# Row maxima and row sums of an attention from PSUM, in turned 32x32 blocks, in place of extra matmuls

## The chip, the cores and the metric

The kernel runs on one core of a Trainium2 chip. The metric is the device time of one execution in microseconds (us), the median of several runs; less is better. The profile comes from one execution on the chip.

## The reference, cut to what matters

A retention layer (a decaying linear attention, `_attn_ref`) gives `x` of shape (4, 768, 512). On it stands a mixture of four attention experts. Each expert is a causal softmax attention with head size 64, and the two experts with the largest gate are mixed.

```python
for e in range(E):                       # E = 4, S = 768, Hd = 64
    q = x @ wq[e]; k = x @ wk[e]; v = x @ wv[e]
    scores = scale * (q @ k.transpose(0, 2, 1))
    causal = np.triu(np.ones((S, S), dtype=bool), 1)
    scores = np.where(causal, -1000000000.0, scores)
    scores = scores - scores.max(-1, keepdims=True)
    a = np.exp(scores)
    a /= a.sum(-1, keepdims=True) + 1e-09
    ye = a @ v @ wo[e]
    for kk in range(K):                  # K = 2, topk from x @ w_gate
        mask = topk[:, :, kk] == e
        out += mask[..., None] * w[:, :, kk:kk + 1] * ye
```

## The kernel before, in words

**Tiling.** Each of the 4 sequences is cut into two halves of 384 rows; the 8 halves are numbered j = 0 to 7 (`NJ`). A half has 3 chunks of 128 rows (`CH`, `C`). The experts come in two pairs p, with e = 0 or 1 inside a pair. An odd half attends to 6 blocks of 128 keys (its own 3 and the 3 of the half before it), an even half to 3.

**Three streams.** `stream_r` runs the retention, chunk after chunk (`h1`, `h2`: L336, L340, L395, L401, with VectorE work on L350, L366 and L409). `stream_p` projects half j to queries and keys (`proj`, 12 matmuls of 384 columns each on L567, split by ScalarE and VectorE into a high part k1 and a low part q2/k2, L572 and L575, and moved between partitions by DMAs issued by SP on L584), makes values and gate logits (`vgate`, L609), the row maxima (`mpass`, `mrow`) and the gate (`gate`, `gate2`). `stream_a` does the attention of half j: `score`, `av` (L862), `norm_a` or `norm_last`, `wout` (L975). While stream r is at half s, stream p is at s-1 and stream a at s-2; the last two attentions follow at the end.

**Row maxima before.** `mpass(j, p, e, i)` multiplies the 128 queries of chunk i with the keys, so that the queries lie on the partitions: L690 (384 keys of the half before, odd halves, i > 0), L703 (the same for i = 0), L704 (the own (i + 1) * 128 keys). VectorE takes the maximum along the free dimension, on L693 with a plain reduction and on L712 with a reduction that also adds the causal mask `cmask`. `mrow` turns the six columns of maxima by a matmul with the identity (L740), ScalarE takes them negated to SBUF (L742), and two DMAs of SP bring them to row 64 of q2 (L744, L746). For j = 7 `mrow` does it by matmuls instead (L733, L736).

**Scores before.** `score(j, p, kb)` multiplies with the keys on the partitions and the queries along the free dimension. Each bank gets two matmuls per expert: L816 (k1 with q1, 128 rows) and L817 (k2 with q2, 65 rows: the low parts, and a row of ones in k2 against the negated maxima in q2). ScalarE takes the exponential into `pt` (L823). GpSimd zeroes the upper triangle of diagonal blocks (L829) and adds the key blocks up into `ac` (L838, L845; VectorE for j = 7). `norm_f` sums `ac` over the partitions by 24 matmuls of 128 columns with a selector `sel` (L886); VectorE adds 1e-9, takes the reciprocal and multiplies with the gate weights (L892, L896, L897). DMAs spread the result (L908, L912).

**What sets the order.** All work is recorded as operations with an engine and dependencies. A tuple `ORDER` written into the file says in which order they are issued (each engine executes its own in that order), and `SLOTS` which buffer of each ring an operation uses. Six PSUM banks form the ring `ps`, which projections, values, retention, maxima, scores and outputs share; one more bank is `ps_o` (output of `av`), one `ps_st` (retention state).

## Time and profile before

| what | us |
|---|---|
| median of 3 runs | 322.73 (322.45 to 324.85) |
| profiled execution: span from first to last instruction | 321.6 |
| profiled execution: its own time | not listed apart; the runs' median is 1.1 above the span |
| TensorE matmuls busy (PE) | 314.9 |
| VectorE busy (DVE) | 175.6 |
| GpSimd busy (POOL) | 167.9 |
| ScalarE busy (ACT) | 128.7 |

In the rows below PE is TensorE's matmuls, PEld its weight loads, DVE VectorE, ACT ScalarE, POOL GpSimd, SP the engine that issues the DMAs. A row of a group gives line, engine, operation, output<-input, shapes, count, then busy time in us, mean ns of one, and the idle time of the engine before them with what ended it. Matmuls overlap in their pipeline, so the mean of one is longer than the distance from one to the next; the chain of waits gives that distance.

### The profile page before, as it was taken

How to read it: one execution, taken by the hardware profiler on the slowest of the kernel's cores; microseconds unless marked ns; L12 is line 12 of the kernel's file. 1: busy time of each engine (PE TensorE's matmuls, PEld its weight loads, DVE VectorE, ACT ScalarE, POOL GpSimd, SP SyncE). 2: the span in 40 equal slices, each digit the busy share in tenths (PEclk: the TensorE clock that was granted, in tenths of full speed). 3: DMA queues.
4: the chain of work that ended last, by engine and by line, in shares of the span. 5: the costliest groups of instructions: out<-in, count | busy, mean ns of one | idle time of the engine just before them, and what ended most of it. 6: DMA issues, size and time to landing. Idle time of an engine off the chain costs nothing.

```text
span 321.6 us, 10842 instructions
## 1 busy us (share of the span) xinstructions
PE 314.9 (98%) x4552; PEld 272.5 (85%) x4552; DVE 175.6 (55%) x465; ACT 128.7 (40%) x322; POOL 167.9 (52%) x205
## 2 busy tenths in 40 slices
PE   8899999999999999999999999999999999999995
PEld 3699998889978799979978789987979798987764
DVE  1672675868344166765323453865525325886842
ACT  1242323343534334342535233334344433547643
POOL 1647232665893904581479923393198454562500
PEclk9999999999999999999999999999999999999999
DMA  7996677844846518440767624843622413435022
GB/s 272 312 395 192 190 225 201 240 119 154 229 128 218 212 45 244 98 129 2 215 173 234 245 96 93 231 139 100 240 73 61 108 28 104 132 106 169 0 99 101
DMA packets 22501, 51.07 MB, mean 159 GB/s; under 512 B 3794, under 2 KB 8742, under 8 KB 22452
## 3 DMA queue, kind: packets, MB, share of 16 engines
q1 hardware_dynamic: 22452, 50.38, 51.2%
q8 instruction: 36, 0.59, 0.8%
q14 instruction: 13, 0.11, 0.1%
HBM read 30.99 MB, written 6.79 MB: 117 GB/s over the span
## 4 chain that ended last, share of the span: by engine, by line
PE 95%; DMA 2%; SPq 1%; DVE 0%; issue 0%; ACT 0%; ACTq 0%
PE ps L567 21%; PE ps L609 11%; PE ps_o L862 11%; PE ps L975 11%; PE ps L816 7%; PE ps L817 7%; PE ps_st L336 5%; PE ps L401 5%; PE ps L704 4%; DMA qkT_t<-in_qkT_dram 2%; PE ps L886 2%; PE ps L690 2%; PE ps L395 2%; PE ps L340 2%; PE ps_st L862 1%; PE ps L703 1%
## 5 line engine op out<-in xcount | busy, mean ns | idle before, releaser
L823 ACT ACTIVATE pt<-ps 128x384 f32<-128x384 f32 (+2 forms) x112 | 50.2, 490 | 29.4 <-PE ps L817 26.4
L829 POOL TENSOR_SCALAR_AFFINE_SELECT pt<-pt 128x256 f32<-128x256 f32 x48 | 19.7, 419 | 67.9 <-ACT pt L823 67.5
L712 DVE CUSTOM_DVE_ANT_0 scr<-ps,cmask_t 128x128 bf16<-128x128 f32 (+3 forms) x64 | 30.2, 486 | 26.6 <-PE ps L704 25.9
L567 PE MATMUL ps<-xh,qk_hi 128*128 128x384 f32 x128 | 43.9, 343 | 0.0
L816 PE MATMUL ps<-q,k 128*128 128x384 f32 (+2 forms) x144 | 43.5, 317 | 0.0
L817 PE MATMUL ps<-q,k 65*128 65x384 f32 (+2 forms) x144 | 42.7, 313 | 0.5 <-issue 0.5
L567 PE MATMUL ps<-xh,qk_lo 128*128 128x384 f32 x128 | 43.1, 337 | 0.0
L567 PE MATMUL ps<-xl,qk_hi 128*128 128x384 f32 x128 | 43.1, 336 | 0.0
L845 POOL TENSOR_TENSOR ac<-ac,pt 128x256 f32<-128x256 f32 (+2 forms) x32 | 39.9, 1249 | 2.2 <-ACT pt L823 0.6
L350 DVE TENSOR_TENSOR sblk<-ps_st,sdec_t 128x256 f32<-128x256 f32 x38 | 16.0, 420 | 42.3 <-PE ps_st L336 34.1
L862 PE MATMUL ps_o<-pt,vt 128*64 128x384 f32 (+2 forms) x252 | 35.8, 422 | 0.0
L572 ACT ACTIVATE k<-ps 128x384 fp32r<-128x384 f32 x32 | 15.4, 488 | 43.4 <-PE ps L567 43.4
L290 POOL TENSOR_TENSOR qd<-qkT_t,qdec_t 128x512 f32<-128x512 f32 (+1 forms) x21 | 25.4, 1212 | 9.7 <-PE ps L340 5.0
L862 PEld LDWEIGHTS ps_o<-pt,vt 128*64 128x64 f32 x252 | 16.5, 136 | 15.3 <-issue 11.9
L816 PEld LDWEIGHTS ps<-q,k 128*128 128x128 f32 x144 | 27.3, 190 | 2.2 <-issue 1.2
L817 PEld LDWEIGHTS ps<-q,k 65*128 65x128 f32 x144 | 27.3, 190 | 0.9 <-issue 0.7
L609 PE MATMUL ps<-vg_hi,xh 128*128 128x260 f32 x96 | 27.7, 289 | 0.0
L275 POOL TENSOR_TENSOR kv_t<-kv_t,kdec_t 128x512 f32<-128x512 f32 (+1 forms) x21 | 20.3, 966 | 14.2 <-DMA kv_t<-in_kv_dram 14.1
L609 PE MATMUL ps<-vg_hi,xl 128*128 128x260 f32 x96 | 27.2, 283 | 0.0
L609 PE MATMUL ps<-vg_lo,xh 128*128 128x260 f32 x96 | 27.1, 282 | 0.0
L363 ACT ACTIVATE xh<-ps 128x512 fp32r<-128x512 f32 x21 | 12.4, 596 | 35.4 <-PE ps L340 33.5
L340 PE MATMUL ps<-qd,sblk 64*64 64x64 f32 x624 | 25.9, 221 | 0.0
(127 smaller groups left out, 774.9 us busy)
## 6 DMA issues: line engine op xcount, KB each, us to landing
qkT_t<-in_qkT_dram SPq DMA_DIRECT2D x24, 512.0 KB
kv_t<-in_kv_dram SPq DMA_DIRECT2D x24, 512.0 KB
out_dram<-ot SPq DMA_DIRECT2D x23, 256.0 KB
q<-k SPq DMA_DIRECT2D x28, 192.0 KB
k<-q SPq DMA_DIRECT2D x14, 192.0 KB
k<-k SPq DMA_DIRECT2D x14, 192.0 KB
fe<-fd SPq DMA_DIRECT2D x28, 96.0 KB
pt<-in_wqk_dram SPq DMA_DIRECT2D x4, 256.0 KB
```

What stands on the lines that cost most here:

```text
L275: e.tensor_tensor(kk, kk, K["kdec"][:, 2 * c:2 * c + n, :, None].to_broadcast([128, n, HP, D]), op=OP.mult)
L290: e.tensor_tensor(halves(qd.t), halves(qb.t[:, 0]), K["qdec"][:, :, None, :].to_broadcast([128, HP, n, SC]), op=OP.mult)
L340: nc.tensor.matmul(yo(m, rt, s), SB[m % 2][rows(rt), s], LD[g, 2].t[rows(rt), s, m % 2 * SC:(m % 2 + 1) * SC], start=m % 2 == 0 and s == 0 ...
L567: nc.tensor.matmul(pb.t[:, :HS], ww[:, kt, wsl], xx[:, kt], start=n == 0, stop=n == 11)
L609: nc.tensor.matmul(pb.t[:, :NV + E], xx[:, kt, sl], ww[:, kt], start=n == 0, stop=n == 11)
L712: lambda: nc.vector.tensor_tensor_reduce(scr.t[:, :n1], pb.t[:, :n1], K["cmask"][:, HS + C - n1:], 1.0, mx0.t[:, e, i:i + 1] if prior else ...
L816: nc.tensor.matmul(o, k1.t[:, e, ko:ko + C], q1.t[:, e, q0:], start=True, stop=False)
L817: nc.tensor.matmul(o, k2.t[:65, e, ko:ko + C], q2.t[:65, e, q0:], start=False, stop=True)
L823: lambda es=es, sb=sb, n=n: nc.scalar.activation(pt.t[:, es[0]:es[0] + n, q0:], sb.t[:, :n * w].rearrange("p (e t) -> p e t", e=n), AF.Exp ...
L845: op(eng, cost, lambda: en.tensor_tensor(ac.t[:, :, q0:], ac.t[:, :, q0:], pt.t[:, :, q0:], op=OP.add), r=[(pt, 0), (pt, 1), (ac, "b")], w ...
L862: nc.tensor.matmul(ob.t[e * 64:e * 64 + 64, q0:HS], vt.t[:, ko // C, ee * 64:ee * 64 + 64], pt.t[:, e, q0:], start=kb == 0, stop=kb == las ...
L975: nc.tensor.matmul(wb.t[:, :n1 - n0], oo[:, sl], ww[:, p, n0:n1], start=n == 0 and p == 0, stop=n == 2 and p == NP - 1)
```

## The change

In halves 0 to 6 the extra matmuls for the row maxima are gone. The score matmuls are cut in two passes. `first` runs the 128-row product of a whole bank (the blocks of a half are packed into banks of up to 512 columns by `banks`), VectorE subtracts 2^100 above the diagonal in PSUM, and a reduction with `apply_transpose=True` takes the maximum in 32x32 blocks turned on the way: each group of 32 keys and 32 queries gives 32 maxima, one per query. `rowmax` joins these over key blocks and partition quadrants in five small VectorE operations, and writes a 32-row diagonal of negated maxima into rows 64 to 95 of q2. `second` adds the low-part product, now with 96 rows, ScalarE takes the exponential, and the row sums come from VectorE by turned reductions of `pt` (even halves) or of `ac` (odd halves, after five GpSimd additions per expert). `norm_a` turns 48 columns of sums with one matmul in place of 24, and VectorE finishes on [48, 32] numbers. GpSimd's triangle zeroing (L829) is gone for these halves. Half 7 keeps its maxima as before, with its own `cmask` written on the chip in place of a DMA; its additions are split per expert. `gate` does part of its work in PSUM and on GpSimd; `gate2` has nine or five more DMAs (one to DRAM, the rest back to [48, 32]). The retention's `wide_y` stays in PSUM. `ORDER` and `SLOTS` are all new (11 buffers of 512 columns for `pt`, 4 for `ac`).

```diff
+MASK_PE = (False, False)
...
+    PT = tag("pt", 11, [128, 512])
+    AC = tag("ac", 4, [128, 512])
+    PM = [tag("pm0", 1, [128, 2, 3, 12]), tag("pm1", 2, [128, 1, 7, 12])]
+    RM = tag("rm", 2, [128, 2, 24])
+    SZ = tag("sz", 1, [128, E, 3, 12])
+    SM = tag("sm", 2, [128, E, 12])
...
+            v.tensor_copy(lp, lg)
+            v.tensor_reduce(mx, lg, axis=AX.X, op=OP.max)
+            v.tensor_tensor(gg.t, lj, li, op=OP.is_gt)
+            v.tensor_tensor(ge.t, lj, li, op=OP.is_equal)
+            v.tensor_tensor(c4(1), lp, mx[:, :, None].to_broadcast([128, NC, E]), op=OP.subtract)
...
+            pl.tensor_tensor(eq.rearrange("p c a b -> p c (a b)"), eq.rearrange("p c a b -> p c (a b)"),
+                             K["gtri"][:, None, :].to_broadcast([128, NC, E * E]), op=OP.mult)
+            pl.tensor_tensor(gt, gt, eq, op=OP.add)
+            pl.tensor_tensor(gt[:, :, :, :2], gt[:, :, :, :2], gt[:, :, :, 2:], op=OP.add)
+            pl.tensor_tensor(gs.t[:, 0], gt[:, :, :, 0], gt[:, :, :, 1], op=OP.add)
+
...
+        def f4():
+            w, sm = gs.t[:, 3], c4(2)[:, :, 0]
+            v.scalar_tensor_tensor(w, gs.t[:, 0], 1.5, c4(1), op0=OP.is_lt, op1=OP.mult)
+            v.tensor_reduce(sm, w, axis=AX.X, op=OP.add)
+            v.tensor_scalar(sm, sm, 1e-9, None, op0=OP.add)
+            v.reciprocal(sm, sm)
+            v.tensor_tensor(wnb.t[:, :, :NC].rearrange("p e c -> p c e"), w,
+                            sm[:, :, None].to_broadcast([128, NC, E]), op=OP.mult)
...
+        op("SP", 0.4, lambda: nc.sync.dma_start(wd.t, wt.t), r=[(wt,)], w=[(wd,)], new=[wd], nbytes=65536)
+        for half in range(2 if b < B - 1 else 1):
+            for e in range(E):
+                def spread(half=half, e=e):
+                    row = wd.t[e * 32 + half * CH:e * 32 + half * CH + CH].rearrange("c (x y) -> (c x) y", y=32)
+                    nc.sync.dma_start(wf.t[e * 12:e * 12 + 12, half], row)
+
...
+    def banks(j):
+
+        def seg(e, kb, col, q0, w):
+            return (e, kb, col, q0, w, kb - j % 2 * CH == q0 // C)
+
+        if j == NJ - 1:
+            u = [[seg(e, kb, 0, 0, HS)] for kb in range(4) for e in range(2)]
+            return u + [[seg(e, kb, e * w, HS - w, w) for e in range(2)] for kb, w in ((4, 256), (5, 128))]
+        if j % 2 == 0:
+            return [*([seg(e, 2, 0, 256, C), seg(e, 0, C, 0, HS)] for e in range(2)),
+                    [seg(0, 1, 0, C, 256), seg(1, 1, 256, C, 256)]]
+        u = []
+        for e in range(2):
+            u += [[seg(e, 0, 0, 0, HS)], [seg(e, 5, 0, 256, C), seg(e, 3, C, 0, HS)],
+                  [seg(e, 2, 0, 256, C), seg(e, 1, C, 0, HS)], [seg(e, 2, 0, 0, 256), seg(e, 4, 256, C, 256)]]
+        return u
+
...
+    def halves(j, p, bank, sb, which):
+
+        for i, (e, kb, col, q0, w, _) in enumerate(bank):
+            kj, ko = kslot(j, kb)
+            q, k, n = (QT[j, p][which], KT[kj, p][which], (128, 65 if j == NJ - 1 else 96)[which])
+            nc.tensor.matmul(sb.t[:, col:col + w], k.t[:n, e, ko:ko + C], q.t[:n, e, q0:q0 + w],
+                             start=not which and not i, stop=bool(which) and i == len(bank) - 1,
+                             skip_group_check=True)
...
+        op("PE", mm_cost(bank) + (len(diag) * C * COL if on_pe else 0), fn,
+           r=tok1(j, p, bank) + ([("nid",), ("cneg",)] if on_pe else []), w=[(sb,)], new=[sb], mode="128x128")
+        if diag and not on_pe:
+            op("DVE", dve_c(C * len(diag)),
+               lambda: nc.vector.tensor_tensor(at(sb.t), at(sb.t), mask().bitcast(F32), op=OP.subtract),
+               r=[(sb,), ("cneg",)], w=[(sb,)])
...
+        def red():
+            x, src, k = pm.t.rearrange("p e r c -> p e (r c)"), blocks(sb.t[:, :w]), n % 4
+            if half:
+                y = (x[:, 0, 72:], x[:, 0, 8:24], x[:, 0, 32:48],
+                     x[:, 0, 48:80].rearrange("p (u c) -> p u c", u=2)[:, :, :8])[k]
+            else:
+                y = x[:, n, 8:24] if n < 2 else x[:, :, 28:]
+            if len(y.shape) == 3:
+                src = src.rearrange("p (u c) y -> p u c y", u=2)
+            nc.vector.tensor_reduce(y, src, axis=AX.X, op=OP.max, apply_transpose=True)
+
+        op("DVE", dve_c(w), red, r=[(sb,), ("pm",)], w=[(pm, n)], new=new)
...
+        def along(r, dst):
+            nc.vector.tensor_reduce(dst.rearrange("p (e c) -> p e c", e=ne), pm.t[r].rearrange("p e r c -> p e c r"),
+                                    axis=AX.X, op=OP.max)
+
+        rd = [(pm, n) for n in range(e * 4, e * 4 + nb)]
+        op("DVE", 0.25, lambda: along(slice(64, 128), rm.t[64:, 0, :nw]), r=rd, w=[(rm, "s")], new=[rm])
+        op("DVE", 0.25, lambda: along(slice(0, 64), at(slice(0, 64), 0)), r=rd + own, w=[(z, "p")],
+           new=[] if half else [z])
+
+        def across():
+            v = nc.vector
+            v.tensor_tensor(rm.t[:32, 1, :nw], at(slice(32, 64), 0), rm.t[96:, 0, :nw], op=OP.max)
+            v.tensor_tensor(at(slice(0, 32), 1), at(slice(0, 32), 0), rm.t[64:96, 0, :nw], op=OP.max)
+            v.tensor_tensor(at(slice(64, 96), 2), at(slice(0, 32), 1), rm.t[:32, 1, :nw], op=OP.max)
+
+        op("DVE", 0.5, across, r=[(z, "p"), (rm, "s")] + own, w=[(z, "m"), (rm, "t")])
+
+        def ex(x):
+            m = at(slice(64, 96), 2)[:, (0 if half else x) * 12:][:, :12]
+            nc.vector.tensor_tensor(q2.t[64:96, x].rearrange("p (c y) -> p c y", y=32),
+                                    m[:, :, None].to_broadcast([32, 12, 32]),
+                                    nid[64:96, None, 64:96].to_broadcast([32, 12, 32]), op=OP.mult)
+
+        for x in es:
+            op("DVE", dve_c(HS), lambda x=x: ex(x), r=[(z, "m"), ("nid",)] + own, w=[(q2, "m", x)])
...
+        op("PE", mm_cost(bank), lambda: halves(j, p, bank, sb, 1), r=tok2(j, p, bank) + [(sb,)], w=[(sb,)],
+           mode="128x128")
+        pt = expo(j, p, n, sb)
...
+            def fn():
+                d, src = y(), blocks(t.t[:, :w])
+                if len(d.shape) == 3:
+                    src = src.rearrange("p (u c) y -> p u c y", u=2)
+                nc.vector.tensor_reduce(d, src, axis=AX.X, op=OP.add, apply_transpose=True)
+
+            op("DVE", dve_c(w), fn, r=rd, w=[tok], new=new)
...
+        add(0, 512, b1, b3, 0, 0, [ac])
+        add(C, 256, ac, b4, C, 0)
+        add(256, 256, ac, b4, 256, 256)
+        add(C, HS, ac, b2, C, 0)
+        add(HS, C, ac, ac, HS, 0)
...
+        op("PE", 0.06, lambda: nc.tensor.transpose(pb.t[:48, :128], s4.t.rearrange("p e c -> p (e c)"), K["ident"]),
+           r=rd + [("ident_t",)], w=[(pb,), (f, "n")], new=[pb, f], mode="128x128")
+
+        def fin():
+            v, x = nc.vector, pb.t[:48, 128:160]
+            v.tensor_reduce(x, pb.t[:48, :128].rearrange("p (g b) -> p b g", g=4), axis=AX.X, op=OP.add)
+            v.tensor_scalar(x, x, 1e-9, None, op0=OP.add)
+            v.reciprocal(x, x)
+            v.tensor_tensor(f.t[:48, :32], x, wf.t[:, half], op=OP.mult)
+
...
+            if j < NJ - 1:
+                bk = banks(j)
+                nb = len(bk) // (1 + j % 2)
+                for e in range(1 + j % 2):
+                    ns = range(e * nb, e * nb + nb)
+                    for n in ns:
+                        u.append((mm_cost(bk[n]), lambda p=p, n=n: first(j, p, n), (j, p)))
+                    if wl:
+                        u.append(wl.pop(0))
+                    u.append((0, lambda p=p, e=e: rowmax(j, p, e)))
+                    for n in [ns[1], ns[2], ns[3], ns[0]] if j % 2 else ns:
+                        u.append((mm_cost(bk[n]), lambda p=p, n=n: second(j, p, n)))
+                for kb in range(nkb):
+                    u.append((4 * w(kb) * COL, lambda p=p, kb=kb: av(j, p, kb)))
+                continue
```

## Rows read from the trace of the kernel before

**Rows 1.** The page: busy time of each engine, share of the span, instructions.
```profile
PE 314.9 (98%) x4552; PEld 272.5 (85%) x4552; DVE 175.6 (55%) x465; ACT 128.7 (40%) x322; POOL 167.9 (52%) x205
```
**Rows 2.** The page: the chain of waits that ended last, its shares by line.
```profile
PE ps L567 21%; PE ps L609 11%; PE ps_o L862 11%; PE ps L975 11%; PE ps L816 7%; PE ps L817 7%; PE ps_st L336 5%; PE ps L401 5%; PE ps L704 4%; DMA qkT_t<-in_qkT_dram 2%; PE ps L886 2%; PE ps L690 2%; PE ps L395 2%; PE ps L340 2%; PE ps_st L862 1%; PE ps L703 1%
```
**Rows 3.** Busy time by stretch: PE, PEld, DVE, ACT, POOL (instructions), granted clock, DMA share, GB/s.
```profile
40.00:300.00 260.00, 259.47 (x3758) 228.04 (x3752) 145.58 (x399) 107.63 (x270) 146.01 (x165) 1.00 0.50 148
55.00:60.00 5.00, 5.00 (x35) 4.04 (x34) 4.25 (x11) 0.75 (x3) 4.83 (x7) 1.00 0.72 227
280.00:300.00 20.00, 20.00 (x149) 15.14 (x149) 16.24 (x36) 12.35 (x29) 10.13 (x14) 1.00 0.37 111
315.00:321.60 6.60, 3.38 (x22) 2.74 (x22) 1.61 (x6) 1.80 (x6) 0.00 (x0) 0.91 0.34 122
```
**Rows 4.** Groups of TensorE: the matmuls of the maxima and of the sums.
```profile
L704 PE MATMUL ps<-k,q x96: 218/287/446, 38.3 to 292.8; 128*128 128x128 f32 x32, 128*128 128x256 f32 x32, 128*128 128x384 f32 x32
L886 PE MATMUL ps<-ac,sel x192: 272/273/297, 71.9 to 308.1; 128*32 128x128 f32 x192
```
**Rows 5.** The chain of waits in order of time: start, length, what.
```profile
56.24 0.11 PE ps L740
56.35 0.52 PE ps L690 x3
56.87 1.45 PE ps_o L862 x12
58.69 0.06 PE ps L704
...
121.28 0.12 PE ps L704
...
147.73 0.79 PE ps L886 x24
```
**Rows 6.** Groups of VectorE and their shapes.
```profile
L712 DVE CUSTOM_DVE_ANT_0 scr<-ps,cmask_t 128x128 bf16<-128x128 f32 (+3 forms) x64 | 30.2, 486 | 26.6 <-PE ps L704 25.9 <-issue 0.5
L575 DVE TENSOR_TENSOR q<-ps,k 128x384 fp32r<-128x384 f32 x32 | 17.3, 551 | 10.3 <-ACT k L572 10.3
L712 DVE CUSTOM_DVE_ANT_0 scr<-ps,cmask_t,mx 128x256 bf16<-128x256 f32 (+1 forms) x32 | 17.1, 548 | 11.9 <-PE ps L704 11.3
L693 DVE TENSOR_REDUCE mx<-ps 128x1 f32<-128x384 f32 x32 | 16.9, 551 | 8.6 <-PE ps L690 8.4
L350 DVE TENSOR_TENSOR sblk<-ps_st,sdec_t 128x256 f32<-128x256 f32 x38 | 16.0, 420 | 42.3 <-PE ps_st L336 34.1 <-PE ps L340 5.4 <-PE ps L401 2.7
L712 DVE DVE_READ_ACCUMULATOR2_ANT mx<- 128x1 f32 x96 | 7.9, 82 | 0.0
L896 DVE RECIPROCAL f<-f 128x128 f32<-128x128 f32 x8 | 7.6, 949 | 0.2
L897 DVE TENSOR_TENSOR f<-f,wt 128x128 f32<-128x128 f32 x8 | 3.5, 435 | 0.3
L892 DVE TENSOR_SCALAR f<-ps 128x128 f32<-128x128 f32 x8 | 2.3, 290 | 6.7 <-PE ps L886 4.0 <-ACT pt L823 2.7
```
**Rows 7.** The same view, shapes kept apart: VectorE's masked maximum over 512 columns, its small operations.
```profile
L712 DVE CUSTOM_DVE_ANT_0 scr<-ps,cmask_t 128x512 bf16<-128x512 f32 x16 | 10.8, 683 | 0.3 <-PE ps L704 0.2
L644 DVE TENSOR_REDUCE gs<-gg 128x24 f32<-128x96 f32 x4 | 1.0, 253 | 0.1
L657 DVE TENSOR_SCALAR gs<-gs 128x6 f32<-128x6 f32 x4 | 0.7, 185 | 0.1
```
**Rows 8.** One line of the gate on VectorE: ns min/median/max.
```profile
L640 DVE TENSOR_TENSOR ge<-lg x4: 251/620/1325, 45.1 to 272.2; 128x96 f32<-128x96 f32 x4
```
**Rows 9.** Groups of GpSimd: zeroing and additions.
```profile
L845 POOL TENSOR_TENSOR ac<-ac,pt 128x256 f32<-128x256 f32 (+2 forms) x32 | 39.9, 1249 | 2.2 <-ACT pt L823 0.6
L838 POOL TENSOR_TENSOR ac<-pt,pt 128x512 f32<-128x512 f32 (+1 forms) x14 | 21.2, 1514 | 7.3 <-ACT pt L823 7.2
L829 POOL TENSOR_SCALAR_AFFINE_SELECT pt<-pt 128x256 f32<-128x256 f32 x48 | 19.7, 419 | 67.9 <-ACT pt L823 67.5 <-PE ps L609 0.3
```

## The prediction

> **What bounds the kernel now.** I read the page's busy times first, then the chain of waits, the stretches, and last the groups of the lines that the change touches. The reader should see that TensorE is the bound: its matmuls are busy for 314.9 of 321.6 us [rows 1], from 40 to 300 us for 259.5 of 260 at the full granted clock [rows 3], and the chain that ended last consists almost wholly of its lines [rows 2]. A matmul taken away therefore gives back its distance to the next one, if nothing else starts to hold TensorE up. VectorE is busy for 145.6 of these 260 us, 0.56 of the time. In the densest stretches it stands at 16.24 of 20 and 4.25 of 5 us, 0.81 and 0.85, and TensorE has no gap there [rows 3]. GpSimd and ScalarE are at about half [rows 1]. All waits of VectorE for TensorE in the groups (26.6 us before L712) cost nothing.

> **The change part by part.**

> *Maxima on TensorE, removed.* Distances come from the chain in order of time [rows 5]: 384 columns take 0.52 / 3 = 0.175 us, 256 columns 0.12, 128 columns 0.12 alone and 0.06 behind a wide one in the same pass. An even half needs 0.12 + 0.12 + 0.175 = 0.415 per expert, times 4 experts and 4 halves, 6.6 us. An odd half has three more of 384 columns: (0.175 + 0.06) + (0.175 + 0.12) + (0.175 + 0.175) = 0.88 per expert, times 12, 10.6. The 14 turnings of L740 at 0.11 are 1.5. Together 18.7 us.

> *Sums on TensorE, removed.* 24 of the 192 matmuls of L886 [rows 4] take 0.79 us [rows 5]; seven halves give 5.5.

> *Added on TensorE.* Seven turnings of sums at 0.11 are 0.8. The scores keep their columns; only block 2 of an odd half is cut in 256 + 128, for 12 experts and two passes: 24 times 0.12 + 0.12 - 0.175, 1.5 us, or nothing by the 0.06 of a short one behind a wide one. The same cut in `av` adds four instructions six times: nothing if columns alone count, 24 x 0.12 = 2.9 if each instruction costs the mean of 1.45 / 12 [rows 5]; I take 1, nearer to columns, since that pack mixes three widths. The net is 18.7 + 5.5 - 0.8 - 1.5 - 1 = 20.9 us, between 18 and 24.

> *VectorE, removed.* Of L712 all but half 7 goes: 30.2 us less 4 x 0.68, plus three quarters of 17.1, plus 7/8 of the 7.9 us of accumulator reads; of L693 three quarters of 16.9; of L892, L896 and L897 together 7/8 of 13.4 [rows 6, 7]. That is 27.5 + 12.8 + 6.9 + 12.7 + 11.7 = 71.6 us.

> *VectorE, added.* No row shows a turned reduction or an operation from PSUM to PSUM. From below I price a turned reduction like the plain one: 0.55 for 384 columns [rows 6], 0.68 for 512 [rows 7], a slope of 1.03 ns per column. From above I take two passes over the columns (rival three). I take the lower, nearest row. Masks are priced like L350 with 256 columns, 0.42 [rows 6] (a 128-column one 0.29 by the slope), the joins by small operations of 0.25 and 0.19 [rows 7], the diagonal of maxima like L575 with 384 columns, 0.55.
> An even half has per pair 3 maxima (2.05), 3 masks (1.26), the join (2 x 0.25 + 3 x 0.19 + 2 x 0.55 = 2.2) and 3 sums (2.0): 7.5; two pairs and 1.1 for the end of the sums make 16.1. An odd half has per expert 4 maxima (2.6), masks of 0.71, the join 1.6 and one sum 0.55: 5.5; four experts and 0.8 make 22.7. Four even and three odd halves: 132.5 us. The gate loses about 9 us on its operations (4 calls; two-operand compares such as L640 [rows 8] now read PSUM).
> Operations on VectorE overlap by some 0.05 us (16.9 us of L693 are 32 x 0.55, but the page's busy time counts each moment once). With 316 operations added and 213 removed that takes 5 us off. The net is 132.5 - 71.6 - 9 - 5 = 47 us, so VectorE goes from 175.6 to about 222, and in the middle of the kernel from 145.6 of 260 to 192 of 239 us, 0.80. That is the density at which rows 3 show TensorE without a gap. So I cost this at little: 3 us of waits in all, bounded by 0 below; the upper bound is rival two. If this cover is gone, each us that VectorE is late is a us of TensorE, since the second pass stands in TensorE's own queue behind the join, and projections and retention behind it.

> *The new wait.* Before, the maxima were made ahead of the scores. Now three or four banks of the six-bank ring are held from the first pass over 3 to 4 us of maxima and masks and 1.6 to 2.2 of joins to the exponential. What is queued behind the second pass on TensorE is the rest of the new order; what waits for banks are projections, gate logits and retention.

> *GpSimd, ScalarE and SP.* GpSimd loses 7/8 of L829 and all its additions of L838 and L845 [rows 9], 17.2 + 61.1 us, and gains five additions for each of 12 experts, at 1.25 us per mean one of L845 at most 75 and by columns about 51, and a few us of the gate. It stays at or below its 167.9. ScalarE's exponentials are packed in fewer instructions. SP loses 28 small DMAs of the maxima and one load, and gains 32 small ones for the gate weights (9 in three sequences, 5 in the last), which wait for the gate and stand ahead of loads in SP's queue; they are hidden by `norm_a`, which needs them only after the whole attention. Half 7 and the end from 300 us stay as they were, with TensorE idle for half of the last 6.6 us [rows 3].

> [...] L640 takes 251 ns at best and 1325 at worst on the same 96 columns [rows 8], while plain reductions from PSUM stay near 551. [...]

> *Sum.* 322.7 - 20.9 + 3 = 304.8; I say 304. The span would be 303, as the median lies 1.1 above the span of the profiled execution.

> **The rivals.**

> *Two: banks and round trips.* The joins sit between the passes 20 times (8 pairs of even halves, 12 experts of odd ones). If each costs TensorE half a us, that is 10 us more: 313. For it: an odd half holds four of six banks for at least 5 us, while TensorE's share of a group is about 8.7 us (35 us a stage over 4). Against it: rows 3 show 0.85 with no gap.

> *Three, slower: the turned reduction takes two passes.* 48 of 512 columns in even halves and 60 of 384 or 512 in odd ones read 52,000 columns; at 1.03 ns each a second pass is 54 us. VectorE would then need 192 + 54 = 246 us in the middle, at a density of 0.9 273 us in place of 260: 322.7 + 13 = 336. It decides from 1.03 + 0.8 ns per column on, where 192 + 42 = 234 us at 0.9 fill the old 260. For it: no row shows the operation. Against it: both plain kinds, L693 and L712, go at one slope.
> [...]

> *Four, slower: the clock.* TensorE ran at full clock in the whole middle, and at a mean of 0.91 only where it was busy for 3.38 of 6.6 us [rows 3]. If the waits of rival two brought that level to the middle, 239 us of work would take 239 / 0.91 = 263, 24 more than by rival two less its own overlap: about 334.
> [...]

> *Five: nothing.* The saved columns come back whole as waits: 322.

> **How the numbers follow.** Chances: forecast 0.63 (own range 298 to 309, from the 18 to 24 us and 0 to 5 us of waits), rival two 0.20 (309 to 320), three 0.10, four 0.04, five 0.03. One per cent, 3.2 us, is what a measurement of this kernel can tell. Faster: 0.63 + 0.19 = 0.82; same: 0.04; slower: 0.14. The range runs from 297 to 321; left out are rivals three, four and a little at the lower end.

> **What would show it.** In the profile after, L690's and L703's successors should be left with 8 and 4 matmuls, L704's with 12, the 128-column sums of L886 with 24; TensorE busy at about 294 us with no gap over a few tenths; a turned reduction of 512 columns at 0.65 to 0.7 us; VectorE at about 222 us. A turned reduction over 0.9 us, a granted clock under 1 in the middle, or waits of TensorE for the joins that sum to over 10 us would make the prediction wrong.

## The result and the profile after

The changed kernel takes 310.56 us (median) where the kernel before took 323.02 beside it: a ratio of 0.960, 95% interval 0.955 to 0.965, so 12.5 us less. It was timed once more for the experiments, with a ratio of 0.962 (0.957 to 0.966). The forecast was 304.0 with a range from 297 to 321: the direction and the range held, but a third of the expected 18.7 us did not come.

The profiled execution took 308.61 us, at the short end of its runs, with a span of 306.9 us at full clock. First the page: busy time of each engine, the instruction loads' DMA queue, and the chain by engine.

```profile
PE 294.9 (96%) x4305; PEld 254.2 (83%) x4305; DVE 229.9 (75%) x565; ACT 121.7 (40%) x283; POOL 148.2 (48%) x201
...
q8 instruction: 34, 0.56, 0.7%
...
PE 90%; issue 3%; DVE 2%; DMA 2%; POOL 1%; ACT 1%; SPq 0%; POOLq 0%; DVEq 0%; ACTq 0%
```

TensorE has 247 matmuls and 20 us of busy time less than in [rows 1], VectorE 54 us more, GpSimd 20 less. TensorE is still the bound, and "issue", idle time for which the profile shows no releaser, has 3% of the chain. The stretches of [rows 3] again:

```profile
40.00:300.00 260.00, 255.16 (x3624) 221.34 (x3620) 210.85 (x529) 109.08 (x254) 126.73 (x158) 1.00 0.53 153
55.00:60.00 5.00, 5.00 (x33) 4.91 (x31) 4.16 (x13) 1.63 (x4) 0.00 (x0) 1.00 0.64 184
```

VectorE went from 145.58 to 210.85 of 260 us, 0.81, and TensorE from 0.5 us of gaps to 4.8. Groups with shapes kept apart: on VectorE the operations that no row of before showed, on TensorE the new turnings of the sums (L1124) and what is left of L886 of [rows 4] (L1092):

```profile
L911 DVE TRANSPOSE_TENSOR_REDUCE pm<-ps 128x16 f32<-128x512 f32 x60 | 39.8, 694 | 1.3 <-PE ps L837 0.7
L977 DVE TRANSPOSE_TENSOR_REDUCE sz<-pt 128x16 f32<-128x512 f32 x24 | 16.3, 694 | 0.3
L952 DVE TENSOR_TENSOR q<-ps,nid 32x384 fp32r<-32x384 f32 x28 | 15.0, 553 | 0.7
L892 DVE TENSOR_TENSOR ps<-ps,cneg 128x256 f32<-128x256 f32 x36 | 14.7, 424 | 5.2 <-PE ps L837 5.1
L911 DVE TRANSPOSE_TENSOR_REDUCE pm<-ps 128x12 f32<-128x384 f32 x12 | 6.9, 577 | 3.5 <-PE ps L837 3.5
L977 DVE TRANSPOSE_TENSOR_REDUCE sm<-ac 128x12 f32<-128x384 f32 x12 | 6.2, 552 | 0.1
L934 DVE TENSOR_REDUCE rm<-pm 64x12 f32<-64x84 f32 x12 | 3.6, 303 | 0.3
L946 DVE TENSOR_TENSOR ps<-ps,rm 32x12 f32<-32x12 f32 x12 | 2.1, 176 | 0.4
L1124 PE MATMUL ps<-ident_t,sm 128*48 128x128 f32 x7 | 1.9, 274 | 0.0
L1092 PE MATMUL ps<-ac,sel 128*32 128x128 f32 x24 | 1.6, 283 | 0.2 <-DVE ac L1052 0.2
L650 DVE TENSOR_TENSOR gg<-ps,lg 128x96 f32<-128x96 f32 x4 | 1.0, 257 | 0.0
L651 DVE TENSOR_TENSOR ge<-ps,lg 128x96 f32<-128x96 f32 x4 | 1.0, 247 | 0.0
```

A turned reduction of 512 columns takes 694 ns, where the plain masked one takes 683 [rows 7]; the mask 0.424, the diagonal 0.553, the join's operations 0.30 and 0.18.

The next table shows where TensorE's time went, summed over the distances from each matmul's start to the next one's, between the first and the last matmul of either trace (us). A distance far above the usual one of its kind is counted as a gap for what lies above it:

```
                                     before   after
maxima (L704, L690, L703 / L724...)   23.2      4.4
score passes (L816, L817 / L837)      44.7     48.8
sums and turnings (L886, L740 / ...)   5.4      0.9
everything else                      230.9    231.5
gaps                                  12.8     16.0
first to last matmul                 317.05   301.56
```

So TensorE's work fell by 18.7 us, the gaps grew by 3.2, and 0.8 us more lay outside. The totals of the last line are firm; how they are divided depends on where a gap begins, and with other limits the gaps grow by 1.6 to 4.6 us. The gaps are the surprise. This is all idle time before TensorE's matmuls from 40 to 300 us, by what ended it (us in total, times, longest), first in the kernel before, then in the changed one:

```profile
PE ps L817 <- issue: 0.5, 1, 0.5
```

```profile
PE ps L400 <- issue: 2.2, 2, 1.2
PE ps_o L1069 <- DVE on L1178: 0.7, 1, 0.7
PE ps L571 <- issue: 0.5, 1, 0.5
PE ps_st L341 <- issue: 0.5, 1, 0.5
PE ps_st L1069 <- DVE on L1178: 0.4, 1, 0.4
PE ps L837 <- ACT lg L627: 0.3, 1, 0.3
PE ps L1092 <- DVE ac L1052: 0.2, 1, 0.2
```

In the changed kernel 3.2 of its 4.8 us of gaps have no releaser; the two waits for L1178 stand behind 295 us, near the end. The pieces without a releaser in the chain, in order of time (start, length, what):

```profile
52.09 0.89 PE ps L571 x5
52.98 0.55 issue
53.53 5.64 PE ps L571 x31
...
64.95 0.10 PE ps L406 x2
65.05 1.18 issue
66.23 0.21 PE ps L400
...
88.66 0.05 PE ps L406
88.72 1.05 issue
89.77 0.27 PE ps L400
...
186.15 0.51 issue
```

The first stands inside a projection of 36 matmuls, five of which had run, the others between matmuls of a retention step. The chain of the kernel before has one such piece, of 0.53 us.

### The profile page after: what moved, and what is told of

It is laid out like the page before. It is cut to its first block, busy times and chain, and to the rows that moved or that the text cites. A ratio compares the mean times of both kernels' runs of the same rounds, so it can differ in the third digit from the quotient of the medians.

```text
span 306.9 us, 10405 instructions
## 1 busy us (share of the span) xinstructions
PE 294.9 (96%) x4305; PEld 254.2 (83%) x4305; DVE 229.9 (75%) x565; ACT 121.7 (40%) x283; POOL 148.2 (48%) x201
## 4 chain that ended last, share of the span: by engine, by line
PE 90%; issue 3%; DVE 2%; DMA 2%; POOL 1%; ACT 1%; SPq 0%; POOLq 0%; DVEq 0%; ACTq 0%
PE ps L571 22%; PE ps L837 15%; PE ps L613 11%; PE ps_o L1069 11%; PE ps L1202 10%; PE ps_st L341 5%; PE ps L406 5%; PE ps L400 2%; PE ps L345 2%; DMA qkT_t<-in_qkT_dram 2%; PE ps_st L1069 1%; PE ps L447 1%; PE ps L474 1%; DVE ac L1052 1%; POOL ol L1153 1%
## 5 line engine op out<-in xcount | busy, mean ns | idle before, releaser
L837 PE MATMUL ps<-q,k 128*128 128x384 f32 (+8 forms) x312 | 56.8, 314 | 0.3 <-ACT lg L627 0.3
L854 ACT ACTIVATE pt<-ps 128x512 f32<-128x512 f32 (+2 forms) x92 | 47.2, 566 | 22.0 <-PE ps L837 19.8
L837 PEld LDWEIGHTS ps<-q,k 128*128 128x128 f32 (+2 forms) x312 | 47.1, 189 | 4.1 <-issue 0.5
L911 DVE TRANSPOSE_TENSOR_REDUCE pm<-ps 128x16 f32<-128x512 f32 (+1 forms) x72 | 46.5, 675 | 4.8 <-PE ps L837 4.2
L571 PE MATMUL ps<-xh,qk_lo 128*128 128x384 f32 x128 | 43.2, 337 | 0.5 <-issue 0.5
L571 PE MATMUL ps<-xh,qk_hi 128*128 128x384 f32 x128 | 43.6, 341 | 0.0
L571 PE MATMUL ps<-xl,qk_hi 128*128 128x384 f32 x128 | 43.1, 336 | 0.0
L1069 PE MATMUL ps_o<-pt,vt 128*64 128x384 f32 (+2 forms) x276 | 35.7, 400 | 0.7 <-DVE on L1178 0.7
L1069 PEld LDWEIGHTS ps_o<-pt,vt 128*64 128x64 f32 x276 | 17.9, 136 | 16.6 <-issue 11.8
L997 POOL TENSOR_TENSOR ac<-ac,pt 128x256 f32<-128x256 f32 (+1 forms) x36 | 29.4, 824 | 1.4
L613 PE MATMUL ps<-vg_hi,xh 128*128 128x260 f32 x96 | 27.5, 287 | 0.0
L997 POOL TENSOR_TENSOR ac<-pt,pt 128x512 f32<-128x512 f32 x12 | 15.4, 1284 | 25.0 <-ACT pt L854 24.9
L341 PE MATMUL ps_st<-kv_t 64*64 64x64 f32 x608 | 25.7, 221 | 0.5 <-issue 0.5
L400 PE MATMUL ps<-am,kv_t 64*64 64x64 f32 x672 | 24.0, 219 | 2.2 <-issue 2.2
L1148 POOL TENSOR_TENSOR on<-on,fe 128x384 f32<-128x384 f32 x14 | 14.1, 1009 | 24.4 <-DMA fe<-fd 24.4
```

Of the source, the lines that this page charges most:

```text
L341: nc.tensor.matmul(ST[b].t[rows(rt), s * D:(s + 1) * D], kvs(m, 0, s)[rows(rt)], kvs(m, 1, s)[rows(rt)], start=c == 0 and s == 0, stop=Fal ...
L400: nc.tensor.matmul(yo(2 * g + u, rt, s), kvs(u + 2 * g, 1, s)[rows(rt)], amg.t[rows(rt), u, s], start=g % NC == 0 and u == 0 and s == 0, s ...
L571: nc.tensor.matmul(pb.t[:, :HS], ww[:, kt, wsl], xx[:, kt], start=n == 0, stop=n == 11)
L613: nc.tensor.matmul(pb.t[:, :NV + E], xx[:, kt, sl], ww[:, kt], start=n == 0, stop=n == 11)
L837: nc.tensor.matmul(sb.t[:, col:col + w], k.t[:n, e, ko:ko + C], q.t[:n, e, q0:q0 + w], start=not which and not i, stop=bool(which) and i = ...
L854: op("ACT", act_c(w), lambda: nc.scalar.activation(pt.t[:, :w], sb.t[:, :w], AF.Exp, scale=isc), r=[(sb,)], w=[(pt,)], new=[pt])
```

## The experiments

The first theory was: TensorE's columns set the time and VectorE, at 0.81, still lies under cover; what is missing of the gain is TensorE's own. Rivals were VectorE's added time, the wait of the second pass for the joins, and the masks' place.

**The changed kernel again**, without an edit, with more runs.

> The changed kernel once more, unchanged, as the base for the others on the same chip. Both theories: 310 us, within 1.5, and again TensorE gaps of some 5 us in the middle, of which I want to see whether they sit at the same matmuls as in the first profile.

Measured: ratio 0.962 (0.957 to 0.966). Its profiled execution was a longer one, with a span of 311.1 us, and shows what varies: the same four pieces of issue, longer, and behind the first of them a stretch at a lower granted clock.

```profile
52.41 1.96 issue
...
67.50 1.38 issue
...
91.33 1.72 issue
...
189.53 0.65 issue
```

The stretches around the first one (columns as in [rows 3]):

```profile
50.00:55.00 5.00, 3.04 (x66) 2.65 (x59) 4.56 (x12) 0.60 (x1) 3.91 (x7) 0.99 0.47 185
55.00:60.00 5.00, 5.00 (x21) 5.00 (x21) 2.70 (x9) 0.94 (x2) 0.00 (x0) 0.66 0.37 81
```

TensorE was busy for 3.04 of 5 us and then got a mean clock of 0.66: by estimate 5 x 0.34 = 1.7 us more are lost there.

**Masks back on TensorE**, in all seven halves, in the odd ones, in the even ones (48, 24 and 24 more matmuls, and as many operations less on VectorE).

```
-MASK_PE = (False, False)
+MASK_PE = (True, True)      # (False, True)   (True, False)
...
+        elif diag:
+            op("DVE", 0, lambda: None)
```

The last two lines put an empty operation in the mask's place, so that the written order still fits.

> One part of the change undone on VectorE: the 36 masks of 256 and 12 of 128 columns go to TensorE as a matmul of the negated identity with the mask (the file's own switch), 36 x 0.12 + 12 x 0.115 = 5.7 us more of TensorE and 18 us less of VectorE, the order else the same. Theory one (TensorE's columns set the time, VectorE's load is hidden but for 3 to 5 us): 312 to 316. Theory two (VectorE at 0.81 holds TensorE up through joins and banks): 310 + 5.7 - 9 = 306 or less.

> Masks on TensorE in odd halves only: 12 x (0.12 + 0.115) = 2.8 us more of TensorE, 8.6 us less of VectorE. Theory one: 310 to 313. Theory two: 308 or less.

> Masks on TensorE in even halves only: 24 x 0.12 = 2.9 us more of TensorE, 10 us less of VectorE. Theory one: 310 to 313. Theory two: 308 or less.

Measured: 0.982 (0.978 to 0.986), 0.971 (0.967 to 0.975) and 0.976 (0.972 to 0.980), so 7, 3 and 5 us above the changed kernel. The busy line of the first's page (of its longest execution):

```profile
PE 301.2 (94%) x4353; PEld 261.3 (82%) x4353; DVE 215.2 (67%) x517; ACT 122.0 (38%) x283; POOL 147.9 (46%) x201
```

VectorE is 14.7 us lighter, TensorE 6.3 heavier, and the time follows TensorE. The masks on VectorE are part of the gain. All three medians (318.4, 314.0 and 316.0 us) lie above the ranges that theory one gave, by 2, 1 and 3 us; what the masks cost beyond their columns stays open. More matmuls also move the edges described below, which these kernels do not keep apart.

**The sums' turned reductions twice, and cut to 32 columns.** The second leaves out the row sums beyond the first 32 columns of each reduction.

```
+                nc.vector.tensor_reduce(d, src, axis=AX.X, op=OP.add, apply_transpose=True)
```
```
-                d, src = y(), blocks(t.t[:, :w])
...
+                d, src = y(), blocks(t.t[:, :32])
...
```

> Each turned sum of halves 0 to 6 is issued twice, 24 x 0.69 + 12 x 0.55 = 23 us more of VectorE, nothing more on TensorE; VectorE rises from 0.81 to about 0.89 of the middle. Theory one (hidden): 310 to 314. Theory two (VectorE nearly binds): half of it or more comes through, 321 or more.

> The turned sums of halves 0 to 6 read 32 columns in place of 512 or 384 (the row sums are left out but for that part), 24 x 0.5 + 12 x 0.37 = 17 us less of VectorE. Theory one: 307 to 310, since only the small waits can go. Theory two: 301 or less.

Measured: 0.997 (0.994 to 1.001) and 0.958 (0.953 to 0.963). The busy line of each page, the doubled one first:

```profile
PE 298.5 (93%) x4305; PEld 254.8 (79%) x4305; DVE 252.8 (79%) x601; ACT 122.3 (38%) x283; POOL 147.9 (46%) x201
```

```profile
PE 294.9 (95%) x4305; PEld 254.4 (82%) x4305; DVE 215.0 (69%) x565; ACT 121.6 (39%) x283; POOL 148.0 (48%) x203
```

Taking 15 us from VectorE gives nothing beyond the intervals: the cover that the prediction counted on was there. Adding 23 us costs some 11, as theory two said for that run and not theory one, so no 23 us of cover are left. Whether the first of the added us cost nothing was not tried; that VectorE lies just under the point from which it decides fits both runs and is not shown.

**The second pass without the join.** The diagonal is written to a tile that nobody reads, so the subtraction of the row maximum is left out and no matmul waits for a join.

```
-            nc.vector.tensor_tensor(q2.t[64:96, x].rearrange(...
+            nc.vector.tensor_tensor(SCR.tiles[0][64:96, :HS].rearrange(...
```

> The diagonal of negated maxima is written to an unused tile, so the second pass of the scores doesn't wait for the joins; VectorE's and TensorE's work is the same (left out: the subtraction of the row maximum). Theory one: the joins are ready when TensorE comes to the second pass, 308 to 311. Rival two of the prediction (half a us of TensorE lost in each of 20 joins): 10 us less than the changed kernel, 300.

Measured: 0.962 (0.958 to 0.966), the changed kernel's own ratio. The 20 round trips through VectorE cost nothing that shows. The changed kernel's trace agrees: it puts no idle time of TensorE before the score matmuls (L837) down to a join.

**The first pass twice**, 132 more matmuls; the second issue writes over the result of the first.

```
             halves(j, p, bank, sb, 0)
+            halves(j, p, bank, sb, 0)
```

> The first score pass of halves 0 to 6 is issued twice into the same bank (the first result is overwritten), about 21 us more of TensorE in the stretch where the removed maxima stood, nothing more on the other engines. Theory one (TensorE is the bound): 310 + 21 = 331, less at most 4 if the present gaps are filled. Theory two (VectorE binds): the extra columns fill TensorE's waits, 318 or less.

Measured: 1.014 (1.009 to 1.019), 17 us above the changed kernel, and its page:

```profile
PE 313.7 (96%) x4437; PEld 273.6 (84%) x4437; DVE 231.6 (71%) x565; ACT 121.9 (37%) x283; POOL 148.0 (45%) x201
```

TensorE's busy time grew by 18.8, so nearly each us of columns is a us of the kernel, as theory one said.

**The pieces of issue.** That left the stalls. Counting matmuls from the first recorded one gave the second theory. In the changed kernel the first matmul behind a stall is number 856, 1109, 1617 and 3139. In the kernel with the masks on TensorE and in the one with the pass doubled it is again number 856 and 1109, though those numbers are other matmuls there (number 856 is a projection on L571, a mask on L886, a score on L837; in the kernel before, a stall precedes number 857, a score). The differences are 253, 508 and 1522: 2, 4 and 12 times 127. The page's queue of instructions moved 0.56 MB in 34 packets, 16 KB each, and 4305 matmuls over 34 loads are 127. And the trace's DMA records show a load landing 1.35 to 1.47 us before each of the four stalls ends. So the theory is that TensorE runs out of instructions at the edge of a load. The next runs shift TensorE's stream against those edges by a longer row of small warm-up matmuls at the start, and change nothing else. The edit for the shift by 28:

```
-            for i in range(12):
+            for i in range(6):
                 nc.tensor.matmul(pbs[i % 6].t, wu, wu[:, None, :].to_broadcast([128, 4, 128]), ...)
+            for i in range(34):
+                nc.tensor.matmul(pbs[i % 6].t[:, :64], wu, wu[:, :64], start=True, stop=True)
```

> The twelve warm-up matmuls of 512 columns become 6 of 512 and 34 of 64: 28 more matmuls at the very start, up to 1 us, and every later TensorE instruction stands 28 matmuls further back in its stream; no work, no order and no dependency of the rest changes. Theory (TensorE's own instructions arrive late): in the profiles so far each middle stall of TensorE without a releaser ends 1.2 to 1.5 us after a 16 KB load of instructions has landed, some 128 matmuls to a load, so the shift puts the edges of the loads at other matmuls: the stalls before L400 at 65 and 89 us and inside L571 at 53 us move or change by over 0.7 us each, and the time changes with their sum, by 1 to 4 us to either side. Rival (the stalls come from the data: banks, VectorE, the joins, the new order's own waits): the same matmuls stall as before, each within 0.5 us, and the time is within 1 us of the changed kernel's, 309 to 312 us, ratio 0.957 to 0.966.

> As with 28, but 1 matmul of 512 columns and 67 of 64, so that the stream is shifted by 56 matmuls, nearly half of a load of instructions. Theory (instructions arrive late): this is about as far from the old edges as a shift can go; the stalls of the changed kernel at 53, 65 and 89 us should be gone or at other matmuls, 3 to 5 us fewer there, others may open where another burst of 64x64 matmuls falls onto an edge; the time differs from the shift by 28 by over 1 us. Rival (data): same matmuls, within 0.5 us, 309 to 313 us.

> As with 28, but all 12 become 96 matmuls of 64 columns, a shift by 84. Theory (instructions arrive late): a third pattern of stalls, and each stall of over 0.6 us between 40 and 280 us again ends 1.2 to 1.7 us after a load of instructions landed; TensorE's work from start to start stays at 285 to 286 us, so the time is that plus the stalls, 305 to 313 us. Rival (data): the old stalls at the old matmuls, 309 to 313 us.

> The warm-up becomes 140 matmuls of 44 columns: a shift by 128 matmuls and their 128 weight loads, 256 instructions, which at 16 KB to a load is one whole load if an instruction has 64 bytes (the loads of the profiles so far stand 127 matmuls apart on average). Theory (late instructions, whose edges are fixed by the position in the stream): a whole load further, the edges fall again where they fall without a shift, so the stalls come back to the matmuls of the unshifted kernel (the 856th, 1109th, 1617th and 3139th matmul of the unshifted count, within 3), 4 to 7 us in all, and those that the shifts by 28, 56 and 84 opened elsewhere are gone; the time is the changed kernel's plus 1 to 3 us for the longer warm-up, 311 to 315 us. Rival (each shift adds its own stalls because the head is later against the loads of data): a fifth pattern, at matmuls that have nothing to do with the unshifted ones.

Measured: 0.969 (0.964 to 0.973), 0.972 (0.968 to 0.975), 0.967 (0.962 to 0.972), and 0.967 (0.963 to 0.970) for the whole load. Every stall of over half a us in the middle, with the number of the first matmul behind it, counted in the kernel's own stream (worked out from the traces; the edges lie at 856 + 126.85 k):

```
kernel          number (us of stall)                                                      sum
changed         856 (0.71) 1109 (1.40) 1617 (1.27) 3139 (0.72)                            4.1
changed, again  856 (2.13) 1109 (1.59) 1617 (1.93) 3139 (0.86)                            6.5
shift 28        1364 (4.44) 2632 (1.23) 2759 (1.09)                                       6.8
shift 56        604 (0.64) 1109 (0.69) 1237 (0.96) 1617 (1.89) 3393 (1.87) 3521 (2.07) 4151 (0.56)  8.7
shift 84        1110 (1.03) 1237 (1.50) 1617 (0.52) 1745 (0.98) 2252 (2.13) 3564 (1.01) 4167 (0.58)  7.8
shift 128       984 (0.72) 1237 (1.65) 1745 (2.93)                                        5.3
```

All but 3564 and 4167 lie within about 3 of an edge, and each ends 1.2 to 1.6 us after a load landed. Most edges pass without a stall. Three of the 28 stalls end within 0.2 us of a releaser that the profile names, and may be waits for data: 1237 of the shift by 56 (VectorE on L911), 4151 and 3564 (a DMA of keys); without them the shifts by 56 and 84 have 7.2 and 6.7 us. The shift by 128 puts them back: 984, 1237 and 1745 less 128 are 856, 1109 and 1617, the matmuls of the unshifted kernel; the fourth is there too, with 0.45 us. (Left out of its row are three distances of L1069 at the lower clock behind the stall before 1745.) So the stalls at edges come from the position in the instruction stream, not from the data. The forecasts of the times were the weaker part: 313.7 us for the shift by 84 lies above 305 to 313, and the shifts by 28 and 56 differ by 1.0 us, which the intervals don't part. The time did not improve: besides other stalls the longer warm-up brings the work behind it 0.2 to 2.3 us later, and the clock pays as well. In the chain of the shift by 28:

```profile
76.03 4.22 issue
80.25 0.27 PE ps_st L341
```

and the stretches around it (columns as in [rows 3]):

```profile
75.00:80.00 5.00, 1.03 (x68) 0.89 (x60) 1.04 (x3) 0.37 (x1) 4.77 (x6) 1.00 0.55 197
80.00:85.00 5.00, 4.75 (x26) 4.68 (x27) 3.12 (x10) 0.60 (x1) 1.99 (x2) 0.66 0.02 5
```

TensorE was busy for 1.03 of 5 us for want of instructions, and the granted clock was 0.66 in the next five. The clock does not fall behind every long stall: in the kernel with the sums cut short TensorE was busy for 2.82 of 5 us around a stall of 2.4 us, less than the 3.04 above, and kept the full clock.

```profile
65.00:70.00 5.00, 2.82 (x136) 2.56 (x132) 1.81 (x4) 0.78 (x2) 2.29 (x3) 1.00 0.99 291
70.00:75.00 5.00, 5.00 (x37) 5.00 (x36) 4.78 (x13) 1.26 (x4) 0.00 (x0) 1.00 0.81 244
```

No run here beats the changed kernel beyond the intervals. What sets how early a load starts was not tried: in the changed kernel it starts 2.3 to 2.8 us before its stall ends and takes 0.9 to 1.3 us. A retention step of 128 matmuls, a whole load with their weight loads, is through in 2.0 us, and 16 of the 28 stalls of the table stand inside such a step; that a load is overtaken there is an argument, not a test. It cannot be the whole cause: in the longest stall, the 4.44 us of the shift by 28, the load itself started 1.8 us after TensorE's last matmul.

## Why the prediction was right, and where it was not

*The bound.* This was right: doubled columns cost what they weigh, and a lighter VectorE gives nothing.

*TensorE's net of 20.9.* It came to 18.7. The maxima gave 18.8 for 17.2, and the cut in `av` cost nothing where 1 us was set. The sums gave 4.0 with their turnings, for 4.7, and L740 0.5 for 1.5: the 0.11 of [rows 5] was the longest of its fourteen distances, the median is 0.027. The term that was mis-sized is the score passes: +4.1 for +1.5. From start to start, a 128-column matmul between wide ones takes 0.06, but the wide one behind it then takes 0.228 in place of 0.177, so the short one's price is 0.11 in all and the 0.06 of [rows 5] was no bound. The 24 cuts are 24 x (0.112 + 0.120 - 0.177) = 1.3 by that; the other 2.8 us lie in the passes' changed order and are not attributed.

*VectorE's prices.* They were right nearly everywhere: 694 ns for 0.68 us, 552 to 577 for 0.55, 424 for 0.42, 553 for 0.55; 229.9 us in all for 222, and 0.81 of the middle for 0.80. Rival three fell with the first row of the groups.

*L640 and the gate.* L650 and L651 now read one operand from PSUM and take 257 and 247 ns on the 96 columns on which L640 took 251 to 1325 [rows 8]. The gate's operations on VectorE went from 17.5 to 7.9 us, 9.6 less where 9 was set. L641, L643 and L644, whose work GpSimd does now, are 4.5 of that; what the operand in PSUM is worth is not shown, since no run moved it alone.

*GpSimd.* L997's additions are 50 us where the bound by columns was 51; the engine ends at 148.2.

*The 3 us of waits.* In the profiled execution the gaps grew by 3.2, so the size was met, but by luck: the prediction laid these waits to VectorE and the banks. The joins cost nothing that shows, a lighter VectorE gave nothing back, and no stall of the changed kernel waits for a bank. What came instead are late instructions, 4.1 us there against 0.7 in the kernel before, and 6.5 in the next profile, there with a clock of 0.66 in 5 us behind the longest. So rival four's lower clock came, as 1.7 us at a single place and not as 24 over the middle, and behind a stall that has no releaser. The prediction had no term for the edges of the stream, and its sign "no gap over a few tenths" failed, with gaps up to 1.4 us in the middle.

*The sum.* By spans it is 321.6 - 18.7 + 3.2 + 0.8 = 306.9, where the forecast had 303. Of these 3.9 us, 2.2 are TensorE's columns, 0.8 the ends, 0.2 the gaps and the rest rounding. The median is 6.6 us off: 0.6 more lies between this execution's span and its time (1.7 to 1.8 in every run here; the 1.1 of the prediction set the median of other executions against this span), and 2.0 between its time and the median. That last part fits the second profile, whose stalls are 2.4 us longer and which lost 1.7 to the clock.

## What to carry to other kernels

Where TensorE is busy for all but a percent, price its matmuls by the distance from start to start and by pairs, and give VectorE work up to the share that hid here, 0.81 of the middle; both came out within a few us. Number the matmuls and compare the idle pieces without a releaser: if the numbers differ by multiples of a load of instructions (127 matmuls here), suspect the instructions before the order and the data, and test it by shifting the stream. A reordering can gain or lose some us by where the edges happen to fall (4 to 7 us of stalls a run in the kernels here). Do not tune for such a gain with one profile: the length of a stall of one kernel differed between two executions by 1.4 us at the same matmul.

## What the runs showed of the hardware

A VectorE load of 0.81 hides behind TensorE in this order (15 us less gained nothing beyond the intervals, 0.958 against 0.960 and 0.962), and of 23 us more half comes through, some 11 us.
